# Widening the guard of a float64-to-float32 conversion: a scale on ScalarE instead of a maximum on VectorE

## The chip, the cores and the metric

The kernel runs on one core of one Trainium2 chip. The metric is the device time of one execution in microseconds (us). The profile names the engines PE (TensorE matmuls), PEld (TensorE weight loads), DVE (VectorE), ACT (ScalarE), POOL (GpSimd) and SP (SyncE, which here only issues transfers).

## The reference

Two attentions between a sequence `x` (8 batches, 8 heads, 512 rows of 64) and a small state (32 rows per head) are computed, their results are joined to 544 rows of 512 per batch, and a feed-forward layer follows:

```python
a = softmax(scale * x @ state.T);  xread = a @ state
a2 = softmax(scale * state @ x.T); sread = a2 @ x
x = concat([xread, sread])         # 8 * 544 rows of 512
h = x @ w_in                       # 512 -> 2048
out = maximum(h, 0) ** 2 @ w_out   # 2048 -> 512
```

`x` and `state` are float32. The two weight matrices arrive as float64, because the set-up multiplies them by a float64 scalar. They reach the kernel as pairs of 32-bit words.

## The kernel before

**Two weight streams.** `w_in` comes in 16 pieces of 128x512 values and `w_out` in 16 more, each 512 KB of word pairs. SP loads them into four buffers shared by both streams (tag `raw`, `RAW = 4`). ScalarE and VectorE turn every piece into float32 with `singles` (line 99 on), in five steps, each reading what the one before wrote. ScalarE writes the absolute value of the high words, read as float32, into the output (line 107). VectorE takes the maximum with 2^-15 (line 108), shifts the bits left by three and masks them (line 109), brings in the sign and the top exponent bit from the high word (line 113), and brings in the top three bits of the low word (line 117). The output is `wf` for `w_in` and `wof` for `w_out`. The high word of a double has eleven exponent bits where a float32 has eight. Read as float32 its exponent field is the upper eight of those eleven, and the shift by three moves the other three to their place. The guard on line 108 keeps small values from giving a wrong exponent.

**What follows a conversion.** A `wof` piece is split (lines 96 to 98) into a high part in the matmul's reduced float format (ScalarE, line 97) and the rest (GpSimd, line 98), called `wo_hi` and `wo_lo`. A `wf` piece is stored back to memory as `wd` from SP's queue (line 162) for later use, split likewise into `w2_0` and `w2_1` (here the rest goes to VectorE), and multiplied by the state (`product`, lines 191 and 203) into `z`, the state times `w_in`. ScalarE moves `z` out of PSUM (line 215) and issues its store to `zd` (line 217). Later SP fetches it (line 230) and it is split into `z_hi` and `z_lo`. The first six `wf` pieces are multiplied unsplit.

**The feed-forward units.** For each batch and each of 16 slices of 128 hidden columns, `up` forms `z` times attention weights (line 392), applies relu (ACT, line 394) and the square (ACT line 396 for the first ten units, DVE line 398 after that), and splits the result into `g_hi` and `g_lo`. `down` multiplies these with `wo_hi` and `wo_lo` (line 418) into four PSUM banks `po`. The first two batches are interleaved while weights still arrive. All the weights are converted for the first units only. After that the six other batches, and at the end the rows of the state, run on weights that lie in SBUF or come back from `zd` and `wd`.

**What sets the order.** The program emits steps in slots. Two lists with due times (`weights` and `reads`) say which loading, converting and attention steps go between the halves of the feed-forward units. A scheduler then orders each engine's instructions by a simulation of the whole program. So an instruction less on one engine lets it place all the others differently. Every engine and every queue executes in the order so fixed, and SP's queue, which issues the loads, also issues the stores of `wd`, each of which waits for its conversion.

Of the kernel before, what the change touches and what calls it, by code (L numbers as in the profile page):

```python
# [9 lines left out]
F32 = mybir.dt.float32  # L10
F32R = mybir.dt.float32r
I32 = mybir.dt.int32
AF = mybir.ActivationFunctionType
# [5 lines left out]
def memory_attention_then_relu2_ffn(  # L19
# [22 lines left out]
    nc = tc.nc  # L42
# [57 lines left out]
    def singles(out_f, words):  # L100

        low, high = words[..., 0], words[..., 1]
        bits = out_f.bitcast(I32)
        nc.scalar.activation(out_f, high.bitcast(F32), AF.Abs)
        nc.vector.tensor_scalar_max(out_f, out_f, 2.0**-15)  # L108
        nc.vector.tensor_scalar(  # L109
            out=bits, in0=bits, scalar1=3, scalar2=0x3FFFFFF8,  # L110
            op0=ALU.logical_shift_left, op1=ALU.bitwise_and,
        )
        nc.vector.scalar_tensor_tensor(  # L113
            out=bits, in0=high, scalar=-0x40000000, in1=bits,
            op0=ALU.bitwise_and, op1=ALU.bitwise_or,
        )
        nc.vector.scalar_tensor_tensor(  # L117
            out=bits, in0=low, scalar=29, in1=bits,
            op0=ALU.logical_shift_right, op1=ALU.bitwise_or,
        )  # L120
# [23 lines left out]
    def z_part(G, k, g):  # L144
# [14 lines left out]
        def convert():  # L159
            wf = sb.tile([P, nq, FW], F32, name="wf", bufs=2)  # L160
            singles(wf, box["raw"])
            nc.sync.dma_start(out=wd[k][:, ccs, :], in_=wf)
            box["wf"] = wf
# [277 lines left out]
    def wo_load(fc):  # L441
        k, i = divmod(fc, FPC)
        raw = sb.tile([P, DM, 2], I32, name="wo_raw", tag="raw", bufs=RAW)
        nc.sync.dma_start(
            out=raw.rearrange("p e w -> p (e w)"), in_=w_out[fc * P:(fc + 1) * P, :]
        )
        wf = sb.tile([P, DM], F32, name="wof", bufs=2)
        singles(wf, raw)
        if i == 0:
            wo[k] = [const.tile([P, FPC, DM], F32R, name=f"{n}{k}") for n in ("wo_hi", "wo_lo")]  # L450
        split(wo[k][0][:, i, :], wo[k][1][:, i, :], wf, nc.gpsimd)
# [161 lines left out]
    for i in range(NGB):  # L613
        pt = ps_x.tile([P, NCC, P], F32, name="pt2", tag="px")
        for cc in range(NCC):
            nc.tensor.transpose(
                out=pt[:, cc, :], in_=sr[i][:, cc * P:(cc + 1) * P], identity=ident
# [60 lines left out]
```

## Time and profile before

| what | before |
|---|---|
| time, median of 3 runs | 716.35 us (716.26 to 717.2) |
| profiled execution's own time | 716.16 us |
| its span, first to last instruction | 714.4 us |
| PE busy | 669.0 us (94%) |
| DVE busy | 465.6 us (65%), 789 instructions |
| ACT busy | 398.2 us (56%), 727 instructions |
| POOL busy | 201.0 us (28%) |
| granted TensorE clock, mean | 0.972 |

The span is what the trace covers. The profiled execution's own time is 1.76 us longer. Busy shares are averages over the whole span, and stages within it differ, so the table of stages has to be read beside them. The granted clock is the share of full TensorE speed that the chip allowed.

### The profile page before, as it was taken

The numbers are of one execution on the slowest core, as the hardware profiler recorded it, in microseconds if no ns is written. First come the engines' busy times: TensorE is split into PE (matmuls) and PEld (weight loads), VectorE is DVE, ScalarE is ACT, GpSimd is POOL, SyncE is SP. The second block draws the span as 40 slices with busy tenths as digits, with TensorE's granted clock in tenths as the row PEclk, the third lists the DMA queues.
The fourth block names the chain that finished last, engine by engine and source line by source line (L and its number), as shares of the span: only waits on it lengthen the run. The fifth ranks groups of instructions, "written<-read, shape, count | busy, mean of one in ns | idle before, by whom it ended". The sixth has DMA issues, their size and how long they took to land.

```text
span 714.4 us, 9776 instructions
## 1 busy us (share of the span) xinstructions
PE 669.0 (94%) x3152; PEld 550.3 (77%) x3152; DVE 465.6 (65%) x789; ACT 398.2 (56%) x727; POOL 201.0 (28%) x181
## 2 busy tenths in 40 slices
PE   3579669999999999999999999999999999999997
PEld 1356457788888888888888878888888888888996
DVE  4969999949655964356955695697954445443453
ACT  3656676667654874367745564565564444442442
POOL 2412442335652460035302331325252022000000
PEclk9589879999999999999999999999999999999999
DMA  8787978733452552144333211322242112100321
GB/s 278 243 273 249 296 229 279 216 118 122 139 185 85 198 186 69 44 149 136 125 100 116 89 60 60 119 89 89 88 132 77 29 30 88 32 16 0 124 84 31
DMA packets 74548, 90.58 MB, mean 127 GB/s; under 512 B 7680, under 2 KB 57600, under 8 KB 74496
## 3 DMA queue, kind: packets, MB, share of 16 engines
q1 hardware_dynamic: 56896, 72.90, 32.5%
q10 hardware_dynamic: 17600, 17.04, 7.1%
q8 instruction: 25, 0.41, 0.2%
q14 instruction: 27, 0.22, 0.1%
HBM read 60.03 MB, written 29.88 MB: 126 GB/s over the span
## 4 chain that ended last, share of the span: by engine, by line
PE 76%; DVE 13%; DMA 7%; issue 2%; ACT 1%; SPq 1%; POOL 0%; DVEq 0%; ACTq 0%
PE po L418 45%; PE ph L392 24%; DMA wo_raw<-w_out 3%; PE pz L203 2%; PE pr L355 2%; DVE wof L113 1%; DMA z_raw<-zd 1%; PE pq L288 1%; DMA w_raw<-w_in 1%; DMA xt_raw<-xT 1%; PE pt L343 1%; DVE wof L117 1%; DVE wf L113 1%; DVE wof L109 1%; DVE wof L108 1%
## 5 line engine op out<-in xcount | busy, mean ns | idle before, releaser
L418 PE MATMUL po<-wo_hi,g_hi 128*128 128x512 f32 x544 | 216.3, 401 | 8.4 <-ACT g_hi L97 5.5
L418 PE MATMUL po<-wo_lo,g_hi 128*128 128x512 f32 x544 | 214.1, 395 | 0.0
L398 DVE TENSOR_TENSOR ph<-ph,r 128x512 f32<-128x512 f32 (+1 forms) x134 | 89.1, 665 | 171.5 <-ACT r L394 171.2
L394 ACT ACTIVATE r<-ph 128x512 f32<-128x512 f32 (+1 forms) x144 | 82.2, 572 | 174.2 <-PE ph L392 173.9
L418 PE MATMUL po<-wo_hi,g_lo 128*128 128x512 f32 x544 | 153.2, 393 | 0.2 <-DVE g_lo L98 0.2
L418 PEld LDWEIGHTS po<-wo_hi,g_hi 128*128 128x128 f32 x544 | 103.8, 191 | 31.1 <-ACT g_hi L97 7.1
L418 PEld LDWEIGHTS po<-wo_lo,g_hi 128*128 128x128 f32 x544 | 103.9, 191 | 19.6
L98 DVE TENSOR_TENSOR g_lo<-ph,g_hi 128x512 fp32r<-128x512 f32 (+1 forms) x144 | 94.4, 656 | 37.0 <-ACT g_hi L97 29.3
L418 PEld LDWEIGHTS po<-wo_hi,g_lo 128*128 128x128 f32 x544 | 102.1, 190 | 21.1 <-DVE g_lo L98 0.7
L97 ACT CAST g_hi<-ph 128x512 fp32r<-128x512 f32 (+1 forms) x144 | 80.8, 562 | 58.9 <-DVE ph L398 50.0
L392 PE MATMUL ph<-a_hi,z_hi 128*128 128x512 f32 x256 | 81.8, 402 | 2.2 <-ACT a_hi L97 1.2
L392 PE MATMUL ph<-a_hi,z_lo 128*128 128x512 f32 x256 | 79.7, 393 | 0.0
L392 PE MATMUL ph<-a_lo,z_hi 128*128 128x512 f32 x256 | 79.3, 390 | 0.0
L98 POOL TENSOR_TENSOR xn_hl<-xn_raw,xn_hl 128x1024 fp32r<-128x1024 f32 x16 | 38.9, 2431 | 138.1 <-ACT xn_hl L97 71.3
L182 POOL TENSOR_TENSOR w<-wf,w 64x512 fp32r<-64x512 f32 x32 | 43.0, 1343 | 71.2 <-ACT w L181 66.4
L392 PEld LDWEIGHTS ph<-a_hi,z_hi 128*128 128x128 f32 x256 | 47.2, 190 | 15.6 <-DVE g_lo L98 3.7
L392 PEld LDWEIGHTS ph<-a_hi,z_lo 128*128 128x128 f32 x256 | 48.2, 189 | 10.8 <-DVE z_lo L98 0.2
L392 PEld LDWEIGHTS ph<-a_lo,z_hi 128*128 128x128 f32 x256 | 47.9, 188 | 10.1
L98 POOL TENSOR_TENSOR xt_hl<-xt_raw,xt_hl 128x1024 fp32r<-128x1024 f32 x12 | 28.8, 2402 | 74.7 <-ACT xt_hl L97 37.0
L98 DVE TENSOR_TENSOR z_lo<-z_raw,z_hi 128x512 fp32r<-128x512 f32 x64 | 47.9, 749 | 0.0
L98 POOL TENSOR_TENSOR wo_lo<-wof,wo_hi 128x512 fp32r<-128x512 f32 x16 | 26.5, 1657 | 53.7 <-ACT wo_hi L97 53.7
L97 ACT CAST z_hi<-z_raw 128x512 fp32r<-128x512 f32 x64 | 39.4, 615 | 1.6 <-DMA z_raw<-zd 1.1
(99 smaller groups left out, 846.5 us busy)
## 6 DMA issues: line engine op xcount, KB each, us to landing
zd<-z_stage ACTq DMA_DIRECT2D x64, 256.0 KB, 2.8
z_raw<-zd SPq DMA_DIRECT2D x252, 64.0 KB, 2.4
xt_raw<-xT SPq DMA_DIRECT2D x16, 512.0 KB, 3.9
w_raw<-w_in SPq DMA_DIRECT2D x16, 512.0 KB, 5.1
wo_raw<-w_out SPq DMA_DIRECT2D x16, 512.0 KB, 4.8
xn_raw<-xn SPq DMA_DIRECT2D x16, 512.0 KB, 3.8
out<-sum SPq DMA_DIRECT2D x32, 256.0 KB, 2.5
wd<-wf SPq DMA_DIRECT2D x16, 256.0 KB, 3.1
```

What stands on the lines that cost most here:

```text
L97: nc.scalar.copy(out=hi, in_=src)
L98: eng_lo.tensor_sub(out=lo, in0=src, in1=hi.bitcast(F32))
L108: nc.vector.tensor_scalar_max(out_f, out_f, 2.0**-15)
L109: nc.vector.tensor_scalar(out=bits, in0=bits, scalar1=3, scalar2=0x3FFFFFF8, op0=ALU.logical_shift_left, op1=ALU.bitwise_and,)
L113: nc.vector.scalar_tensor_tensor(out=bits, in0=high, scalar=-0x40000000, in1=bits, op0=ALU.bitwise_and, op1=ALU.bitwise_or,)
L182: nc.gpsimd.tensor_sub(out=w[other], in0=wf[own], in1=w[own].bitcast(F32))
L203: nc.tensor.matmul(pz[:, q, :], lhsT=a[:, h, :], rhs=w, start=j == 0, stop=j == len(todo) - 1,)
L355: nc.tensor.matmul(pr[:, q].rearrange("p i c -> p (i c)"), lhsT=my["e"][:, t, q].rearrange("p i n -> p (i n)"), rhs=my["xn"][:, t, q].rear ...
L392: nc.tensor.matmul(ph, lhsT=w, rhs=v, start=i == 0, stop=i == len(todo) - 1)
L394: nc.scalar.activation(r, ph, AF.Relu)
L398: nc.vector.tensor_mul(out=ph, in0=ph, in1=r)
L418: nc.tensor.matmul(po[t], lhsT=g, rhs=w, start=i == 0 and j == 0, stop=i == last and j == 2)
```

## The change

The maximum on VectorE goes away. ScalarE's absolute value gets a scale of 2^-112 in the same instruction, so that the exponent field it writes is already lowered by 112 and runs from zero. The two masks widen by one bit each to fit. The number of ScalarE instructions in `singles` stays one, and VectorE's go from four to three.

```diff
         low, high = words[..., 0], words[..., 1]
         bits = out_f.bitcast(I32)
-        nc.scalar.activation(out_f, high.bitcast(F32), AF.Abs)
-        nc.vector.tensor_scalar_max(out_f, out_f, 2.0**-15)
+        nc.scalar.activation(out_f, high.bitcast(F32), AF.Abs, scale=2.0**-112)
         nc.vector.tensor_scalar(
-            out=bits, in0=bits, scalar1=3, scalar2=0x3FFFFFF8,
+            out=bits, in0=bits, scalar1=3, scalar2=0x7FFFFFF8,
             op0=ALU.logical_shift_left, op1=ALU.bitwise_and,
         )
         nc.vector.scalar_tensor_tensor(
-            out=bits, in0=high, scalar=-0x40000000, in1=bits,
+            out=bits, in0=high, scalar=-0x80000000, in1=bits,
             op0=ALU.bitwise_and, op1=ALU.bitwise_or,
         )
         nc.vector.scalar_tensor_tensor(
             out=bits, in0=low, scalar=29, in1=bits,
             op0=ALU.logical_shift_right, op1=ALU.bitwise_or,
         )
```

The absolute value moves from line 107 to line 108 of the file, and the other lines keep their numbers.

The order moves on all engines. Two places follow, each as it was and as it is.

VectorE around the first conversion of a `w_out` piece (`wof`), with `w_in` pieces (`wf`) and a split of `z` beside it, before:

```order
L108 TENSOR_SCALAR wof_262<-wof_262 128x512
L109 TENSOR_SCALAR wof_262<-wof_262 128x512
L108 TENSOR_SCALAR wf_272<-wf_272 128x512
L113 SCALAR_TENSOR_TENSOR wof_262<-wo_raw_260,wof_262 128x512
L98 TENSOR_TENSOR z_lo_235<-z_raw_199,z_hi_234 128x512
L109 TENSOR_SCALAR wf_272<-wf_272 128x512
L117 SCALAR_TENSOR_TENSOR wof_262<-wo_raw_260,wof_262 128x512
L113 SCALAR_TENSOR_TENSOR wf_272<-w_raw_231,wf_272 128x512
```

The same place now:

```order
L109 TENSOR_SCALAR wf_268<-wf_268 128x512
L98 TENSOR_TENSOR z_lo_233<-z_raw_197,z_hi_232 128x512
L113 SCALAR_TENSOR_TENSOR wf_268<-w_raw_229,wf_268 128x512
L109 TENSOR_SCALAR wof_259<-wof_259 128x512
L117 SCALAR_TENSOR_TENSOR wf_268<-w_raw_229,wf_268 128x512
L113 SCALAR_TENSOR_TENSOR wof_259<-wo_raw_257,wof_259 128x512
L109 TENSOR_SCALAR wf_285<-wf_285 128x512
L117 SCALAR_TENSOR_TENSOR wof_259<-wo_raw_257,wof_259 128x512
```

The rows of line 108 are gone, the split of `z` stands ahead of the first `wof`, and a `wf` piece is interleaved with it at each step.

PE at the third feed-forward unit, whose `down` reads `wo_hi1` and `wo_lo1` (L418), with the products `pz` of the seventh `wf` piece (two of them, one per parity of the heads) around it, before:

```order
L203 MATMUL pz_540<-w2_0_435,stz_lo_173 128x256
L203 MATMUL pz_540<-w2_0_435,stz_hi_172 128x256
L203 MATMUL pz_540<-w2_1_436,stz_hi_172 128x256
L418 MATMUL po0_485<-wo_hi1_308,g_hi_419 128x512
L418 MATMUL po0_485<-wo_lo1_309,g_hi_419 128x512
```

The same place now:

```order
L203 MATMUL pz_524<-w2_1_424,stz_hi_172 128x256
L203 MATMUL pz_546<-w2_0_423,stz_lo_173 128x256
L203 MATMUL pz_546<-w2_0_423,stz_hi_172 128x256
L203 MATMUL pz_546<-w2_1_424,stz_hi_172 128x256
...
L418 MATMUL po0_471<-wo_hi1_300,g_hi_407 128x512
L418 MATMUL po0_471<-wo_lo1_301,g_hi_407 128x512
```

Both products of the piece now stand ahead of the third `down`, where before the second one came after it.

## The prediction

> **What bounds the kernel now.** I read the page's totals first, then a table of stages, then who waits for whom. By the totals PE is busy 94% of the span, so a gain can come only from its idle 6% and from slow clock.
>
> ```profile
> span 714.4 us, 9776 instructions
> PE 669.0 (94%) x3152; PEld 550.3 (77%) x3152; DVE 465.6 (65%) x789; ACT 398.2 (56%) x727; POOL 201.0 (28%) x181
> ```
>
> The table of stages (window and its length, then busy us and instructions of PE, PEld, DVE, ACT and POOL, granted clock, share of the DMA engines, GB/s) says where that is:
>
> ```profile
> 0.00:18.00 18.00, 6.63 (x12) 3.06 (x14) 8.82 (x17) 6.92 (x14) 4.96 (x13) 0.94 0.87 279
> 18.00:36.00 18.00, 10.38 (x42) 6.52 (x40) 17.73 (x34) 12.02 (x25) 7.57 (x6) 0.59 0.75 244
> 36.00:54.00 18.00, 13.47 (x43) 9.22 (x44) 11.10 (x21) 10.70 (x20) 2.56 (x2) 0.81 0.85 273
> 54.00:108.00 54.00, 39.27 (x169) 30.31 (x168) 52.78 (x94) 38.09 (x72) 20.68 (x13) 0.87 0.81 257
> 102.00:108.00 6.00, 4.83 (x17) 4.31 (x18) 5.76 (x11) 4.09 (x8) 3.12 (x2) 0.51 0.95 294
> 108.00:144.00 36.00, 34.78 (x160) 27.36 (x159) 35.06 (x54) 22.64 (x43) 12.25 (x8) 1.00 0.75 242
> 144.00:660.00 516.00, 515.19 (x2428) 429.67 (x2427) 315.59 (x524) 286.93 (x507) 152.95 (x141) 1.00 0.30 96
> ```
>
> From 144 to 660 us PE idles 0.8 us in 516: nothing that helps VectorE there helps the kernel. All that can be had lies before. In 18 to 36 and in 54 to 108 VectorE is busy 98% of the time (17.73 of 18, 52.78 of 54) while PE idles 7.6 and 14.7 us. There VectorE sets the pace. In 36 to 54 it has time over (11.10 of 18), and the transfers are the busier resource. In 108 to 144 both are full, and PE idles only 1.2 us.
>
> PE's waits up to 108 us (wait, total us, times, longest) name VectorE, or engines that it feeds:
>
> ```profile
> PE pz L191 <- DVE wf L117: 7.2, 2, 5.2
> PE po L418 <- ACT g_hi L97: 4.4, 2, 3.5
> PE pz L203 <- DVE w L98: 3.2, 2, 2.9
> PE po L418 <- ACT wo_hi L97: 3.0, 1, 3.0
> PE pz L203 <- ACT w L97: 2.6, 1, 2.6
> ```
>
> `wf` on line 117 is the last step of a conversion, and `wo_hi` and the casts of `w` wait for that step too. SP's queue hangs on the same steps. In 54 to 108 its longest wait is a store of `wd` behind a conversion, and every load behind it in the queue is late with it:
>
> ```profile
> SPq L162 <- DVE wf L109: 7.8, 2, 7.6
> ```
>
> **The change part by part: what goes.** The changed line runs 32 times, all before 144 us (the stages of line 108 alone; DVE busy and count come first):
>
> ```profile
> 18.00:36.00 18.00, 2.67 (x4) 0.59 0.75 244
> 36.00:54.00 18.00, 2.12 (x5) 0.81 0.85 273
> 54.00:108.00 54.00, 9.28 (x13) 0.87 0.81 257
> 108.00:144.00 36.00, 4.38 (x8) 1.00 0.75 242
> ```
>
> What is one of them worth? The recorded durations are of two kinds. The timeline (start, us, engine, line) has undisturbed ones, and ones four times as long:
>
> ```profile
> 79.91 0.41 DVE L108 TENSOR_SCALAR wf<-wf 128x512 f32<-128x512 f32 x1
> 80.24 0.68 DVE L98 TENSOR_TENSOR g_lo<-ph,g_hi 128x512 fp32r<-128x512 f32 x1
> 93.66 1.75 POOL L98 TENSOR_TENSOR a_lo<-at,a_hi 128x512 fp32r<-128x512 f32 x1
> 94.17 1.52 DVE L108 TENSOR_SCALAR wof<-wof 128x512 f32<-128x512 f32 x1
> 62.76 1.55 POOL L98 TENSOR_TENSOR wo_lo<-wof,wo_hi 128x512 fp32r<-128x512 f32 x1 [1.76 <-ACT wo_hi L97]
> 63.08 1.52 DVE L109 TENSOR_SCALAR wof<-wof 128x512 int32<-128x512 int32 x1
> ```
>
> An undisturbed one holds VectorE for 0.33 us (80.24 minus 79.91). The long one at 94.17 ends at 95.69, just behind a GpSimd instruction that ran to 95.41. At 63.08 line 109, which stays, is stretched in the same way: it ends at 64.60, with the GpSimd instruction running to 64.31. So the extra time is waiting for GpSimd, and the line behind takes it over when line 108 is gone. I therefore price a removed instruction at 0.33 us. The other bound is its whole recorded time.
>
> [...]
>
> The sum: in the two stages that VectorE sets there are 4 + 13 = 17 instructions, 17 x 0.33 = 5.6 us. In 36 to 54 VectorE is busy 62% (11.10 of 18). I count 62% of 5 x 0.33, 1.0 us, between nothing (the transfers set this stage) and 2.12. In 108 to 144 the 8 instructions are hidden by PE's own work, 34.78 us of 36. If that cover were gone they would be worth 8 x 0.33 = 2.6 us, though no more than the 1.2 us that PE idles. In 0 to 18 VectorE waits more than it works (8.82 of 18), so the two there count nothing. Together 6.6 us.
>
> **What is added.** The absolute value gets a scale. The trace has this instruction without one, and an exponential with an immediate scale on the same shape, both SBUF to SBUF:
>
> ```profile
> L107 ACT ACTIVATE wf<-w_raw 128x512 f32<-128x512 f32 x16 | 10.7, 672 | 15.8 <-DMA w_raw<-w_in 9.3 <-PE pz L191 3.3 <-DVE w L98 3.2
> L317 ACT ACTIVATE q<-q 128x512 f32<-128x512 f32 x16 | 10.1, 628 | 0.7 <-DVE q L316 0.7
> ```
>
> The one with a scale is not longer (628 against 672 ns), so I take zero. ACT has time over in 54 to 108 (38.09 of 54). If the scale cost as much as the difference of these rows, 0.04 us, the 13 + 4 would lose 0.7 us at most. The masks change a constant only, and take zero.
>
> **What is moved.** Both order pairs above show the same: conversions come earlier, and PE takes both products of a `wf` piece before the third `down`. Counted over PE's order, 48 rows of products stand ahead of the fifth `down` now, against 18 before. The same work is done by the end of the front stage, so I count nothing for the move itself. Its bad side is the third rival. What is late next after the stall is gone: the weights' loads, at 0.81 of the DMA engines, which have room for the 7 us of compression (54 x 0.81 / 48 is 0.91). On the clock I count nothing in the sum. PE ran 54 to 108 at 0.87, so at full clock its 39.27 us would be 5.1 us less, and that is the bound.
>
> The profiled execution took 716.16 us, 0.19 under the median, so the forecast is 716.16 - 6.6 = **709.6 us**.
>
> **The rivals.** First, **the transfers hide it.** If loads set the pace in 54 to 108, only the 18 to 36 stage pays, 4 x 0.33 = 1.3 us, and the time is 714.9. For it stands SP's share above and a DMA share of 0.95 in the quoted 6 us stretch; against it, VectorE's 98%, and that SP's longest wait is itself on VectorE.
>
> Second, **the stalls go too.** Then 2.67 + 2.12 + 9.28 = 14.1 us leave and the time is 702.1. For it: fewer instructions of the kind that collides with GpSimd. Against it: line 109 is of that kind and now comes first.
>
> Third, the other side: **PE parks on early products.** PE takes its work in order. With 30 more rows of products ahead of the fifth `down`, it waits at them for `w` while `down` work behind is ready. Two more waits as long as those in PE's list (2.9 and 2.6) are 5.5 us, and a slow-clock stretch behind each, like 102 to 108 (4.83 us at 0.51, half of it lost, 2.4), 4.7 more. That is 10.2 - 6.6 = 3.6 us slower, 719.8. It decides once PE's idle time and lost clock in this stage grow by more than 6.6 us. Against it: the conversions that feed those products come earlier too.
>
> [...]
>
> **How the numbers follow.** The forecast, 705 to 713, has a chance of 0.49; the transfers hide it (713 to 717.5) 0.20; the stalls go too (below 705) 0.14; PE parks (above 717.5) 0.17. A measurement of this kernel can tell about 0.2%, 1.4 us, from no change. Faster by more takes the first and third cases whole and half of the second, 0.73. Within takes the other half of it, 0.10. Slower has 0.17. The range for 8 in 10 goes from 702.0, where recorded durations count whole, to 717.5, where PE's parking would have eaten the gain. The first case's own range is 705 to 713.
>
> **What would show it.** Right: 757 DVE instructions; the absolute value still near 672 ns; line 109's mean rises, because it inherits the stalls, so that DVE's busy time falls nearer to 11 than to 19 us; PE idle in the first 144 us down by about 6 us, and unbroken PE work from about 137 us on instead of 144. Wrong: PE waits at `pz` L203 longer in total than the 5.8 us here, SP's queue waiting for DMA rather than DVE, or a difference that arises after 144 us.

## The result and the profile after

The changed kernel takes 707.56 us (median of 4 runs, 706.96 to 708.43), the kernel before in the same comparison 716.78. The ratio is 0.986, with a 95% interval of 0.984 to 0.988. The forecast was 709.6 us in a range of 702.0 to 717.5. The profiled execution took 708.43 us, 7.7 less than the 716.16 of before. The page's totals after:

```profile
span 706.6 us, 9753 instructions
PE 669.8 (95%) x3152; PEld 551.6 (78%) x3152; DVE 452.2 (64%) x757; ACT 398.3 (56%) x727; POOL 199.3 (28%) x181
```

The 32 maxima are gone (757 instead of 789), and VectorE is busy 13.4 us less. PE does the same matmuls in nearly the same busy time (669.8 against 669.0 us), so the gain is idle time that went away. The table of stages, in the columns of the prediction's table, says where (the two stages from 18 to 54 us are left out here):

```profile
54.00:108.00 54.00, 43.95 (x199) 35.11 (x198) 52.23 (x85) 40.72 (x77) 21.17 (x14) 0.91 0.89 287
108.00:144.00 36.00, 35.43 (x168) 29.38 (x168) 28.03 (x40) 22.54 (x41) 12.25 (x9) 1.00 0.67 212
144.00:660.00 516.00, 514.47 (x2431) 429.25 (x2430) 316.26 (x526) 285.94 (x507) 150.36 (x138) 1.00 0.30 94
```

PE's busy time in 54 to 108 rose from 39.27 to 43.95 us, half of what it gained in the whole front, and VectorE is as full there as it was (52.23 against 52.78). From 144 to 660 us PE is 0.7 us worse. The rest of this text uses one number of each kernel, PE's busy time in the front stage, 0 to 144 us (first column after the window). Before and after:

```profile
0.00:144.00 144.00, 104.53 (x421) 76.46 (x422) 125.50 (x216) 90.38 (x172) 48.02 (x41) 0.87 0.80 256
```

```profile
0.00:144.00 144.00, 113.81 (x463) 85.14 (x464) 114.67 (x189) 94.45 (x178) 48.90 (x43) 0.87 0.82 267
```

PE works 9.3 us more in the front, at the same mean clock. Its idle time there fell by as much, where the prediction had said about 6. Some of PE's waits up to 108 us, one of before that the prediction does not show, and four after the change:

```profile
PE pz L191 <- DVE s L338: 6.7, 1, 6.7
```

```profile
PE pz L191 <- DVE wf L117: 11.7, 4, 4.0
PE pz L203 <- ACT w L97: 2.5, 2, 2.2
PE pz L203 <- ACT e L309: 2.4, 1, 2.4
PE pz L203 <- DVE w L98: 2.0, 2, 1.1
```

All waits of `down` (L418) for `g_hi` and `wo_hi`, 7.4 us before, are gone. At the plain products (L191) the waits for `wf` grew from 7.2 to 11.7. The prediction's list left out two others there, 6.7 us for a softmax step of VectorE (`s`) and 4.9 for `z_stage`. The first is gone and the second is 2.7, so the waits at the plain products fell from 18.8 to 14.4 us in all. PE waits at other places, and less.

### The profile page after: what moved, and what is told of

Its sections match the earlier page's. It is cut to its first block, busy times and chain, and to the rows that moved or that the text cites. A ratio compares the mean times of both kernels' runs of the same rounds, so it can differ in the third digit from the quotient of the medians.

```text
span 706.6 us, 9753 instructions
## 1 busy us (share of the span) xinstructions
PE 669.8 (95%) x3152; PEld 551.6 (78%) x3152; DVE 452.2 (64%) x757; ACT 398.3 (56%) x727; POOL 199.3 (28%) x181
## 4 chain that ended last, share of the span: by engine, by line
PE 79%; DVE 8%; DMA 6%; issue 2%; ACT 2%; SPq 1%; POOL 0%; DVEq 0%; ACTq 0%; POOLq 0%
PE po L418 47%; PE ph L392 25%; PE pz L203 3%; DMA wo_raw<-w_out 2%; PE pr L355 2%; DMA sp_raw<-stP 2%; PE pq L288 1%; PE pt L343 1%; DVE wf L117 1%; DVE wf L113 1%; DVE z_lo L98 1%; DVE g_lo L98 1%; DMA zd<-z_stage 1%; DMA xt_raw<-xT 1%; DVE wf L109 1%
## 5 line engine op out<-in xcount | busy, mean ns | idle before, releaser
L418 PE MATMUL po<-wo_hi,g_hi 128*128 128x512 f32 x544 | 217.3, 400 | 0.6 <-ACT g_hi L97 0.5
L418 PE MATMUL po<-wo_lo,g_hi 128*128 128x512 f32 x544 | 215.0, 395 | 0.0
L418 PE MATMUL po<-wo_hi,g_lo 128*128 128x512 f32 x544 | 152.2, 392 | 0.0
L418 PEld LDWEIGHTS po<-wo_hi,g_hi 128*128 128x128 f32 x544 | 103.9, 191 | 22.4 <-ACT g_hi L97 2.0
L418 PEld LDWEIGHTS po<-wo_lo,g_hi 128*128 128x128 f32 x544 | 103.9, 191 | 19.5
L418 PEld LDWEIGHTS po<-wo_hi,g_lo 128*128 128x128 f32 x544 | 101.5, 189 | 21.1 <-issue 1.0
L392 PEld LDWEIGHTS ph<-a_hi,z_hi 128*128 128x128 f32 x256 | 47.6, 190 | 15.2 <-DVE g_lo L98 2.1
```

The lines of the kernel that those rows point to most:

```text
L392: nc.tensor.matmul(ph, lhsT=w, rhs=v, start=i == 0, stop=i == len(todo) - 1)
L418: nc.tensor.matmul(po[t], lhsT=g, rhs=w, start=i == 0 and j == 0, stop=i == last and j == 2)
```

## The experiments

All times are medians, and each is compared with the kernel before on its own chip and in its own set of runs, where before took 717.5 to 718.2 us. Between sets, which ran on different chips, ratios are compared and not times. The theory was that the VectorE work taken out is the gain, 0.33 us at a time. The rival was that the new order of all engines is the gain. The scheduler makes a new order for every program, so the two come together in the changed kernel and had to be taken apart.

**The scale alone.** The first kernel keeps the scale and the wider masks and puts a full maximum back:

```diff
         nc.scalar.activation(out_f, high.bitcast(F32), AF.Abs, scale=2.0**-112)
+        nc.vector.tensor_scalar_max(out_f, out_f, 0.0)
```

Its order on every engine is that of before, row by row.

> The new scale on ScalarE and the wider masks, with a full maximum (bound zero) put back on VectorE. The order of every engine is that of the kernel before, row by row. If the scale costs ScalarE nothing: 716 to 717.5 us, and the absolute value still takes 672 to 682 ns. If the gain came by way of ScalarE or the masks: 708 us.

It took 717.55 us, ratio 0.9993 (0.9978 to 1.0008). Its group of the absolute value for `w_in` (count, busy, mean ns, then idle before):

```profile
L108 ACT ACTIVATE wf<-w_raw 128x512 f32<-128x512 f32 x16 | 10.8, 678 | 13.6 <-DMA w_raw<-w_in 8.3 <-DMA wd<-wf 4.2 <-DMA z_raw<-zd 1.1
```

678 ns, and 681 for `w_out`, stand against 672 and 677 without the scale. The scale and the masks cost nothing that can be measured, and bring nothing by themselves.

**The work alone, first try.** After the scheduler has set the order, the 32 maxima of that kernel are shrunk to 2 columns, so that the order stays that of before:

```diff
+        GUARDS.append(nc.vector.tensor_scalar_max(out_f, out_f, 0.0).ins)
...
+    resize(nc, lambda ap: [ap[0], [ap[-1][0], 2]])   # after the order is set
```

> Every engine executes in the order of the kernel before, with the new scale on ScalarE. VectorE's maximum keeps its 32 places, but works on 2 of the 512 columns (with a bound of zero, so that it changes nothing). If the removed VectorE work itself is the gain (my theory): 32 instructions shrink from about 0.33 us to under 0.1, so about 80% of the gain of 9.2 us comes, 708 to 711 us. If the gain came from the new order of the engines (rival): nothing moves, 715.5 to 717.5 us. If stalls behind GpSimd go with the instruction: VectorE's busy time falls by 17 us or more against the kernel before; if they are inherited, by 9 to 12.

It took 715.77 us, ratio 0.9966 (0.9955 to 0.9978): 2.4 us of the gain, in the rival's range. The shrunk instructions still cost something:

```profile
L128 DVE TENSOR_SCALAR wf<-wf 128x2 f32<-128x2 f32 x16 | 5.0, 312 | 14.7 <-ACT wf L127 14.5
```

On 2 columns they took 312 ns in the mean for `wf` and 182 for `wof`. VectorE's busy time fell by 8.9 us, from 465.6 to 456.7. So this was no clean test, and two more followed.

**The two corners.** Here each engine is held to a given order by edges that set only which instruction comes before which. One kernel has the changed work in the order of before, with the maxima taken out of VectorE's rows. The other has the order of the changed kernel, with a full maximum put in ahead of each shift. In the traces PE, VectorE and GpSimd run row by row in the order given, but for the maxima. No run holds a kernel by edges to its own order, so what the edges themselves cost was not measured alone. The shrunk maximum, without edges, and the maximum taken out, with edges, have nearly the same ratio (0.9966 and 0.9962).

```diff
+                        prev = tails.get(one.engine)
+                        if prev is not None:
+                            tc.add_manual_dep(
+                                one, prev,
+                                mybir.DependencyInfo(mybir.DependencyClass.NoSync, mybir.DependencyReason.DATA),
...
+                        tails[one.engine] = one.name
```

> The changed kernel's work, with all engines held to the order of the kernel before: VectorE's order is that of before with the 32 maxima taken out, the others are that of before row by row. The shrunk maximum left 2.4 us of gain, and its 32 small instructions still took 182 to 312 ns each. If those remnants hid the gain of the work (my theory, weakened): 709 to 712 us. If the work alone is worth little and the order is most of it (rival): 714 to 716.5 us.

> The other corner: all engines held to the order of the changed kernel, with a full maximum (bound zero) put back on VectorE just ahead of each shift. If the work is what counts: 715 to 718 us. If the order is most of it: 709 to 712 us, some 2 to 4 us above the changed kernel.

> The changed kernel itself, on the chip of the other runs of this set: 706.5 to 709 us by every theory.

| | order of before | order of the changed kernel |
|---|---|---|
| with the maximum | 717.54 us | 721.48 us, ratio 1.0061 (1.0042 to 1.0079) |
| without it | 715.13 us, 0.9962 (0.9944 to 0.9981) | 707.65 us, 0.9868 (0.9848 to 0.9888) |

The theory of the work missed both corners. The rival's range holds the first one (714 to 716.5) and misses the second (709 to 712) by 9.5 us. Taking the work out of the old order brings 2.4 us. The new order with the old work is 3.9 us slower than before. Only the two together bring 9.9. In the new order the same 32 instructions are worth 13.8 us (721.48 - 707.65), in the old one 2.4.

What makes the new order slow with the old work? Its totals and its row of 0 to 144 us:

```profile
PE 676.0 (94%) x3152; PEld 555.0 (77%) x3152; DVE 466.6 (65%) x789; ACT 398.2 (55%) x727; POOL 197.2 (27%) x181
```

```profile
0.00:144.00 144.00, 107.49 (x405) 78.12 (x406) 124.60 (x214) 89.14 (x169) 44.30 (x41) 0.82 0.81 257
```

The span is 719.6 us, so PE idles 43.6 us in all, no more than the 45.4 (714.4 - 669.0) of before. The same 3152 matmuls take 7.0 us longer, at a granted clock in the front of 0.82 against 0.87. All four runs had a mean clock of 0.963 to 0.969, the thirteen of before 0.969 to 0.976. So against the kernel before the loss in this corner is slower matmuls and not longer waits. Against the changed kernel (idle for 36.8 us) both grew, 6.8 us of idle time and 6.2 of busy time. PE's busy time in the front (107.49 us for 405 matmuls, 104.53 for 421 before) is thus a measure of its work only where the clock is the same. The waits changed place from the old order to the new: those at the split products (L206 here, L203 before) came to 13.6 us up to 144 us against 5.8, those of `down` to 1.0 against 8.1. With the maximum gone the split products' waits are 8.4 and the clock is back at 0.87. What lowered the clock in this corner was not tested.

What becomes of the freed time in the old order? In the kernel without the maximum the stage of 54 to 108 us reads:

```profile
54.00:108.00 54.00, 41.44 (x173) 32.73 (x172) 48.01 (x79) 36.85 (x69) 19.06 (x13) 0.84 0.82 259
```

VectorE went from 52.78 to 48.01 us busy and is idle for 6.0 us, since it now reaches instructions whose inputs aren't there: its waits for ScalarE's steps come to 3.9 + 0.9 + 0.6 + 0.6 us in this stage, against 1.0 + 0.2 before. Its largest wait by total in this stage, and the largest in SP's queue in 36 to 144 us, in the same kernel:

```profile
DVE z_lo L99 <- ACT z_hi L98: 3.9, 3, 1.8
SPq L233 <- DMA zd<-z_stage: 16.4, 5, 5.8
```

In the kernel before the same two stretches have no wait of that kind on VectorE. In SP's queue they have the first of these rows, and the changed kernel, run again in this set, has the second:

```profile
SPq L230 <- DMA zd<-z_stage: 10.5, 2, 5.8
```

```profile
SPq L230 <- DMA zd<-z_stage: 15.7, 6, 9.4
```

The fetch of `z` in SP's queue waits 16.4 us for stores of `z` to land, 5.9 more than before. But the changed kernel waits there about as long (15.7 us) and is fast, so this wait does not explain why the old order loses the freed time. What is shown is that VectorE idles here for want of inputs, 6.0 us. In the kernel with the shrunk maximum it idles for 6.6 us in this stage (busy 47.38 of 54). The profiled execution of this kernel, 711.76 us, was the fastest of its ten, which spread to 717.23, and its trace therefore shows more of a gain than the median of 2.4 us.

**Only the transfers' order put back.** The four computing engines keep the changed kernel's order, SP's queue gets that of before.

> The changed kernel, its four computing engines in its own order, and only SP's queue of transfers held to the order of the kernel before. If the new order pays through earlier or better placed transfers: 711 to 716 us. If it pays through what PE, VectorE and ScalarE do in which order: 707 to 709 us.

It took 731.48 us, ratio 1.0194 (1.0169 to 1.0219), slower than anything expected. Its waits in SP's queue and on ScalarE between 50 and 100 us, and on PE up to 150 us, the longest of each:

```profile
SPq L233 <- DVE z_lo L99: 16.3, 2, 14.4
ACT wf L109 <- DMA w_raw<-w_in: 15.2, 1, 15.2
PE pz L206 <- ACT z_stage L218: 15.1, 4, 12.1
```

A fetch of `z` sits 14.4 us at the head of the queue, waiting for VectorE to split an earlier piece of `z`, which stands later in VectorE's new order. Behind it stands a load of `w_in`, for which ScalarE waits 15.2 us in one go. PE's products are parked for 12.1. So the queue's order of before, beside the computing orders of the changed kernel, cost 23.8 us (731.48 - 707.65).

**More and less work in the new order.** In one kernel the shift of line 109 walks the columns with a stride of 256, in the order of the changed kernel. In another the last step of the conversion works on 2 columns, so that the lowest three bits of the weights are left out.

```diff
+    resize(nc, lambda ap: [ap[0], [ap[-1][0], 256], [256 * ap[-1][0], 2]])   # first kernel: line 109
+    resize(nc, lambda ap: [ap[0], [ap[-1][0], 2]])                           # second kernel: line 117
```

> Every engine executes in the order of the changed kernel. The shift of line 109 walks the columns with a stride instead of one after the other, which I expect to cost about 0.2 to 0.35 us more in each of 32 instructions. If VectorE's work is what counts (my theory): about 0.27 x 22 = 6 us slower than the changed kernel, 712 to 715 us. If the order is what counts (rival): 707 to 709 us.

> Every engine executes in the order of the changed kernel. The last step of the conversion, which brings in the lowest three bits from the low word, works on 2 of the 512 columns, so those bits are left out of the weights. That takes about 0.55 us more off VectorE 32 times. If VectorE still sets the pace in the front stage: 17 to 22 of them count, 9 to 12 us, 696 to 699 us. If the transfers, at 0.89 of the DMA engines in 54 to 108 us, are now the bound (rival): a gain of 0 to 4 us, 703.5 to 707.5 us.

The strided shift took 0.29 us more (median 705 and 711 ns against 420), but the time was 710.15 us, ratio 0.9879 (0.9860 to 0.9898). By ratio (the changed kernel has 0.9868 on its chip) that is 0.8 us more than the changed kernel, and the intervals overlap, so the time lies between the two forecasts, nearer to the rival's. The kernel without the last step has 17.8 us less VectorE work on the page (434.4 against 452.2) and took 705.67 us, 0.9822 (0.9798 to 0.9846): 3.3 us less by ratio, in the range that I had given to the transfers. Of the 17.8 us of work taken off VectorE beyond what this order was made for, 3.3 came back as time. Work added cost anything from 0.8 us (0.29 x 32 = 9.3 us of shift) to 13.8 (the maximum, with 14.4 us more on the page, 466.6 against 452.2). The traces show two differences between them: with the slow shift VectorE's busy time rose by 5.4 us only (457.6), and PE took 670.6 us for its matmuls, where with the maximum it took 676.0. More was not settled.

**Orders made for the work.** Four kernels let the scheduler make its own order. One has a maximum that is on 2 columns from the start. Two change only one of the weight streams. The last leaves out the last step of the conversion altogether, and with it the lowest three bits of the weights.

```diff
+        tiny = out_f[:, :2] if len(out_f.shape) == 2 else out_f[:, 0, :2]     # first kernel
+        nc.vector.tensor_scalar_max(tiny, tiny, 0.0)
+        if len(out_f.shape) == 2:   # second kernel: a w_out piece
...                                  # the old conversion, return
+        if len(out_f.shape) == 3:   # third kernel: a w_in piece
...                                  # the old conversion, return
-        nc.vector.scalar_tensor_tensor(                                       # fourth kernel
-            out=bits, in0=low, scalar=29, in1=bits,
...
```

> The scale on ScalarE, and a maximum on 2 of the 512 columns that was already that small when the scheduler ordered the program, so that the order is a third one, made for about the changed kernel's work. If an order made for the smaller work brings the gain whichever it is (theory A, the schedule adapts): 707 to 711 us. If the changed kernel's order is a lucky one (theory B): 712 to 717 us.

> Only the 16 pieces of w_in are converted in the new way, w_out's keep the maximum, and the scheduler orders the program for that. Theory A: 16 of 32 instructions, about half the gain, 711 to 714 us. Theory B: anything from 706 to 720 us, with no relation to the half.

> The other half: only the 16 pieces of w_out are converted in the new way, in the order that the scheduler makes for that. Theory A: 711 to 714 us. Theory B: anything from 706 to 720 us.

> The changed kernel without the last step of the conversion (the lowest three bits of the weights are left out, 32 VectorE instructions of about 0.6 us less), in the order that the scheduler makes for it. In the changed kernel's order the same work came to only 2.0 us. Theory A: the order adapts and more of it comes, 697 to 703 us. If the transfers bound the front stage by now: 703 to 706 us. Theory B: anything, also slower than 708 us.

| kernel, in its own order | time | ratio to before |
|---|---|---|
| maximum on 2 columns | 710.10 us | 0.9895 (0.9871 to 0.9919) |
| new conversion for `w_in` only | 719.05 us | 1.0021 (1.0007 to 1.0035) |
| new conversion for `w_out` only | 716.63 us | 0.9980 (0.9963 to 0.9996) |
| no last step | 697.18 us | 0.9720 (0.9704 to 0.9737) |

The first and the last speak for an order that adapts. A third order for nearly the same work brings 7.5 us. The work of the last step, worth 3.3 us in the changed kernel's order, is worth 10.6 in an order made without it (both by ratio). The halves speak against a smooth relation: half the work brought a loss of 1.4 us with one stream and a gain of 1.0 with the other, where 3.5 to 6.5 had been expected. Both halves miss the range of the order that adapts (711 to 714). If this is the luck of their orders, which is not shown, that luck is as large as the whole effect of half the change. PE's busy time in the front follows the time in these four (107.94, 103.86, 104.82 and 121.63 us in the order of the table). Here are the rows of 0 to 144 us of the `w_in` half and of the kernel without the last step:

```profile
0.00:144.00 144.00, 103.86 (x411) 75.11 (x412) 119.62 (x199) 92.21 (x173) 48.53 (x43) 0.87 0.82 263
```

```profile
0.00:144.00 144.00, 121.63 (x517) 92.44 (x518) 101.75 (x166) 101.78 (x193) 50.56 (x46) 0.92 0.85 273
```

In the first VectorE has 5.9 us less to do than before (119.62 against 125.50) and PE gets no more done. In the second PE gains 17.1 us on before, the span is 19.7 shorter, and the DMA engines are at 0.95 in 54 to 108, so the transfers were not the bound in the changed kernel, which had them at 0.89:

```profile
54.00:108.00 54.00, 50.49 (x244) 41.28 (x244) 47.56 (x76) 45.94 (x87) 21.00 (x15) 0.97 0.95 310
```

No kernel with the full conversion was faster than the changed one.

## Why the prediction was right or wrong

**The time was right, the sum was not.** The forecast of a 6.6 us gain came from work alone, with nothing for the move. Measured with the order held, the work is 2.4 us, and the rest of the 9.9 us of that set, 7.5 us, comes with the move once the work is gone. Taken the other way round, the move costs 3.9 us and the work then brings 13.8, and neither split is the truer one. Two terms were wrong in opposite directions, by 4.2 us too much and 7.5 too little. That they cancelled so far that the time came out inside the forecast is luck.

- *"The same work is done by the end of the front stage, so I count nothing for the move itself."* This is the step that failed. The order was not a side of the change beside its work. It decided whether freed VectorE time became PE time. The rows quoted showed products and conversions coming earlier, and I read them only for a risk.
- *"An undisturbed one holds VectorE for 0.33 us", times 17.* The price of an instruction held roughly: VectorE's busy time fell by 13.4 us, or 0.42 for each of 32. What failed is that those of two stages were counted at full worth because VectorE was 98% busy there. In the old order 2.4 us came of the 6.6 in all, and VectorE then idled for 6.0 us in 54 to 108.
- *"The line behind takes it over."* VectorE's busy time was forecast nearer to 11 than to 19 us lower. It fell by 13.4. The price of 0.33 us gave 10.6, whole records 19.3, so the measurement lies between. The two long records quoted, which end at 95.69 and 64.60 us behind GpSimd instructions that ran to 95.41 and 64.31, spoke for the former. That they wait for GpSimd was my reading of these two, and no run tested it. But line 109 was not the heir. The groups of the conversion that changed most, before and after:

```profile
L109 DVE TENSOR_SCALAR wof<-wof 128x512 int32<-128x512 int32 x16 | 12.9, 805 | 0.1
L109 DVE TENSOR_SCALAR wf<-wf 128x512 int32<-128x512 int32 x16 | 7.4, 465 | 0.2
L117 DVE SCALAR_TENSOR_TENSOR wf<-w_raw,wf 128x512 int32<-128x512 int32 x16 | 11.7, 732 | 0.1
```

```profile
L109 DVE TENSOR_SCALAR wf<-wf 128x512 int32<-128x512 int32 x16 | 10.2, 637 | 9.3 <-ACT wf L108 9.3
L109 DVE TENSOR_SCALAR wof<-wof 128x512 int32<-128x512 int32 x16 | 9.0, 561 | 6.2 <-ACT wof L108 6.2
L117 DVE SCALAR_TENSOR_TENSOR wf<-w_raw,wf 128x512 int32<-128x512 int32 x16 | 13.2, 822 | 0.2
```

  For `wf` line 109 rose from 465 to 637 ns, for `wof` it fell from 805 to 561, and its 32 instructions together took 20.3 us before and 19.2 after. The sign that I had named, a higher mean on line 109, holds for `wf` alone. Line 117 for `wf` rose from 732 to 822. In the old order without the maximum line 109 has 632 and 539 ns, so its shift comes with the removal and not with the move.
- *The scale at zero* was right: 0.9993 (0.9978 to 1.0008) with nothing else changed.
- *In 108 to 144 the work is hidden by PE* is in keeping with the profile: VectorE's busy time fell by 7.0 us there, and PE, which idled 1.2 us, idles 0.6.
- *"A difference that arises after 144 us"* would have counted against it: there PE is 0.7 us worse, 514.47 against 515.19.

**The rivals.** *The transfers hide it* (714.9) did not hold in the changed kernel, and in the kernel without the last step they moved more, 310 against 287 GB/s. *The stalls go too* would have given 702.1 us and did not happen. *PE parks on early products* was right that PE would wait longer at the products (13.6 us against 5.8 in the new order with the old work) and that the clock could fall (0.82 against 0.87 there), and wrong on what the waits cost. It had put the cost of the move at 10.2 us, 5.5 of waits and 4.7 of clock, from which the 6.6 of the work were taken to give 3.6. With the old work in the new order the cost measured alone is 3.9 us, and the trace has it as slower matmuls, with no more idle time. With the smaller work none of it is left in the time. The sign I had named for this rival was a bad one: PE's waits at `pz` L203 for ScalarE and VectorE grew from 5.8 to 8.4 us (2.5 + 2.4 + 2.0 + 1.5), above the bound, while the kernel got faster, because the waits of `down`, 8.1 us before, went away.

**What stays open.** Which part of the new order carries the 7.5 us was not isolated. No run mixes the orders of PE, VectorE and ScalarE one by one. Each corner has one trace, and two executions with the same rows on every engine (the kernel before and the scale alone) differ by 2.0 us of PE's whole busy time and 2.6 of its idle time, so smaller differences of these totals say nothing. That the two halves bring so little is measured, and that it is the luck of their orders is argued only.

## What to carry to other kernels

An engine that is 98% busy in a stage is no proof that its work is worth its time (2.4 us came here of the 6.6 priced): hold the order fixed, take the work out, and see whether it goes idle instead. Read PE's busy time with its clock: in the new order with the old work the idle time was 43.6 us against 45.4, while the same matmuls took 7.0 us longer. Where a scheduler orders the program anew, a change is always work and order together, so price both, and expect to miss by a few microseconds, as both halves did here. Check a queue of transfers against the orders of the engines it waits for: one out of step cost more here (13.9 us over before) than the change itself brought (9.9).

## What the hardware showed that was not expected

A VectorE maximum on 2 of 512 columns took 166 to 170 ns in the median, against some 420 on 512, so shrinking an instruction is a poor stand-in for taking it away. The shift and mask on 32-bit integers went from a median of 420 to 705 ns when it walked the same 512 columns with a stride of 256.
